# Twelve instead of six tiles normalised ahead in a performer-attention and Fourier-mixing kernel

## The chip, the cores and the metric

The kernel runs on one core of a Trainium2 chip. A core has five engines that each work through their own list of instructions in order: PE (TensorE, matrix products), DVE (VectorE), ACT (ScalarE), POOL (GpSimd) and SP (SyncE, which here issues nearly all DMA transfers). They wait for each other by semaphores. The metric is the device time of one execution in microseconds (us); lower is better.

## The reference

The input is `q`, `k`, `v` of shape (8, 8, 576, 64), all in float32. For each of 64 heads the kernel must compute a linear attention with random features, then join the heads to rows of 512 numbers, and on these 8 x 576 = 4608 rows a Fourier mixing block with a two-layer perceptron:

```python
def phi(x):
    proj = np.einsum('bhsd,md->bhsm', x, omega)
    sq = np.sum(x * x, axis=-1, keepdims=True) / 2.0
    h = proj - sq
    h = h - np.max(h, axis=-1, keepdims=True)
    return np.exp(h) / np.sqrt(m)
q_p, k_p = (phi(q_s), phi(k_s))
kv = np.einsum('bhsm,bhsd->bhmd', k_p, v)
...
X = np.fft.fft(x, axis=1)
X = np.fft.fft(X, axis=2)
u = x + np.real(X).astype(np.float32)
mu = np.mean(u, axis=-1, keepdims=True)
var = np.mean((u - mu) ** 2, axis=-1, keepdims=True)
un = (u - mu) / np.sqrt(var + 1e-06)
ch = np.maximum(un @ w_ch1, 0.0) @ w_ch2
return (u + ch).astype(np.float32)
```

`w_ch1` is 512 x 2048, `w_ch2` 2048 x 512.

## The kernel before, in words

The program has two parts. The **first part** does the attention of 32 pairs of heads, the Fourier transforms of the eight batches (as products with cosine and sine tables), and writes the rows `u` to a DRAM tensor `us`. Beside it the weights are converted, and the first 512 rows ("plain" tiles 0 to 3 of 128 rows) go through the perceptron. The **second part** takes the other 4096 rows in eight blocks of 512, j = 0 to 7, through the perceptron, by Strassen's scheme with seven products instead of eight, applied twice. Blocks 0 and 1 go one by one; from j = 2 (`WIDE`) on they go in pairs. Products of the first layer are at L1710 and L1861, of the second at L2153; the seven operand parts of a weight are called leaves, and they are loaded from DRAM into buffers `wl` (second layer, L2049) or `wx`/`wxw` (first layer). There are twelve such buffers, `NWL`.

Before the first layer a block's rows must be normalised and turned, so that tokens lie along the free dimension. Block 0 does that with PE. For blocks 1 to 7, 28 tiles of 128 rows, it is done without PE: load the tile's rows from `us`, two ACT passes for mean and variance, three small POOL operations, an ACT pass that normalises, a DVE transpose in blocks of 32, and a store to a DRAM tensor `turned`, from which the block is fetched later. The 128 rows of such a tile are every other group of 32 of 256 rows; one DMA fetches them by a rearranged pattern (4 groups of 32 rows).

Where this happens: `normed` (second part, L1094) lists it as steps among the others, by `norm_of` and `by_blocks`, with the row load at L1135 and the store at L1074. Six of the 28 tiles (blocks 1 and half of 2, `EARLY`) are done in the first part by `ahead` (L1571), in buffers `kq` that the attention has left; its row load is at L1578, statistics on ACT at L1582 and L1583, POOL at L1585 to L1587, normalisation at L1589, the transpose on DVE at L1592 and the store at L1594.

The order of all engines is written by a planner, `Listing`. Streams of steps (Python generators) wait for events and buffers; each time one step is chosen and its instructions are issued at the end of its engines' lists. The choice is prescribed by strings: `PICKS` and `BANKS` for all 1853 steps of the first part; `PICKS2` and `BANKS2` for the first 1105 steps of the second part (after these the planner chooses by its own clock); `BANKS` names the PSUM bank of each product. The stages of an `ahead` tile are not steps: `BETWEEN` holds groups of five characters, four digits for a step of the first part and one for a tile, and after that step the tile's next stage is issued. A tile has six stages: load, statistics, POOL, normalisation, transpose, store. The first part ends with the eight products of the second layer of plain tile 3 (L1258); the numbers of its last steps are: 1820 the last eviction that ACT does (L1221), 1822 a DVE sum of the last batch, 1835 to 1838 the sums of block 0's tokens on DVE (L1417), 1841 and 1842 stores of rows, 1845 the store of the mirrored rows, 1846 the load of plain tile 3's rows for the residual, 1847 its addition on DVE (L1271), 1848 its store (L1038), 1849 and 1850 copies of the mirrored rows (L1020), 1853 the end.

In the second part the first product starts with two leaf products on PE (L1710); the third adds into a bank that ACT fills with the result of the first (`seed`, L1742). DVE and POOL start with sums of weight parts (L1666).

Memory of the first part is given back before the second (`early.close()`): the leaf buffers of the second part lie where `kq` and `kqT` were.

Of the kernel before, what the change touches and what calls it, by code (L numbers as in the profile page):

```python
# [18 lines left out]
F32 = mybir.dt.float32  # L19
# [22 lines left out]
class Clock(NamedTuple):  # L42
# [60 lines left out]
PICKS2 = (  # L103
    "0260260270280000270290290290260280240261260290310251280251290450480490270451280230480420480290460440"
    "2802602504812504802404704604504704504505105105103812605105002504102404912404804604604802304404904614"
    "9150048048052053049052053053035044049046037052037041028046125037048044048038046037141154052043043060"
    "0400370330330570540351230450370350360270440580570570470550261230420521230280360360480470400440470300"
    "4603803504004202802905005605614815903905705312305906103405804905003705604905905403304903804803303905"
    "2058048051037033046051034039058051046059059025057046038033052035037055039060057043037047045054057045"
    "0410440670571270670690530670440470400510470510490310600460390270390580380500611280630560590620410631"  # L110
    "2715106104904706000005505005405405604315904004704314403205505305315405303204303805712615102603603914"
    "2052040043038041153049064060053022049050040061039047063000050038040049052050051035129054022059137044"
    "0500500370570320370200630560340480200440500471440590600600410580510360420490400550510520610471510590"
    "6203805106006205606005706015705805406115004216005203215606005915705105205405215604805405204804603815"
    "6027022054049028148047043046051045053155147045047024053148043050153043046148021037047055056052037054"
    "1490480520410430501470540470000551520470520490550571471531560470540440440540520490540480440450490320"
    "5104603503914804704005105103204404604004304904405304704005104303304905013903905005104704005204604804"
    "5051052053053053042145045046054141049046153040052040051051046047051048038053143147049053053053053045"
    "0410450240430430410001460420480270360481410440440380390500420400460440410450420310420480420520500440"
    "4204503804205114903604003804703704004802103904504604701803903905403703605405405205605505503703403705"  # L120
    "2055051051054053050053053050053055036029051050035051050044046048051051050046049053053046052044044034"
    "0440480480450430470240320430460451540460460450500471490550410320400480450450000450460430390470470500"
    "4504604104404002204904004702404504004811804004402104103604704503804004104204203502804804603404504704"
    "6048039039037044045042043044042034034040040045042040040039034000052032033044038033016032040027032037"
    "0340430361250290380400330420320360370480390370460290420300350400500370251260490390170360370330410430"
    "3303103203703603802304403803003604502403603504603303202504604103402304403403103003003202604113814103"
    "3030032041032039026034030029127027131027036029027031041045041027029027034142143032020039037027036028"
    "0270400400261340321270320260310310310370370350340300350300331310350340350390390390391360370260360300"
    "3012903703103103513113903403203303903403703203102903303602902313513402903313602403403203512803513403"
    "2135032036033033133031030034032131030031032032132031034035128032028037032038035132032035032026026023"  # L130
    "0300370161270251270270260360271321331360310250310290351300341311331340241330290350251320320290290180"
    "2002201712503102102403102902402803203401803202803302503203112103012802102102203002802003102302702712"
    "6020023026023023124023020023029017027122028027125024023026128030029024021029027021026023029027020125"
    "0230261210261301330250240240260240220320280220300300251250280220250190250300201200270000200260220220"
    "2303303302602801902612402802702502401902912902802802102702402802002702602502302802102601702502102202"
    "8018027026028020020127127127021018023024019000019025014017026027026018024026017014021016020017020016"
    "022017016025024"
)
BANKS2 = (
    "5670712567365475162765765076736574251742053164735260173564271706573527460152371054362071534267053152"  # L140
    "76"
# [223 lines left out]
def kernel(  # L365
# [667 lines left out]

    outs = out.rearrange("b t d -> (b t) d")
# [61 lines left out]
    def normed(j, pool):  # L1096
        t0 = (NPLAIN * TP + TB * j) // 128

        def paced(i):
            h, k = divmod(i, HT // 128)  # L1100
            before, then = ((("first", j - 1, n[i], 0), "y") for n in ((1, 1, 5, 2), (6, 2, 7, 3)))
            if wide(j):

                n, was = i + TB // 128 * (j - head(j)), head(head(j) - 1)
                order_ = [((("first",) + p), "y") for p in heads(was)]
                at = [m * (len(order_) - 2) // 7 for m in range(8)]
                if j <= WIDE + 1:
                    order_ = [(("first", 0, 7, 0), "y"), *((("second", 0, k), "p1") for k in (4, 6))]
                    order_ += [(("first", 1, ORDER1[k], 0), "y") for k in (0, 2, 4, 6)]
                    at = range(-2, 6)  # L1110
                before, then = order_[at[n]], order_[at[n] + 1]
            yield Step(NONE, after=events_of(range(t0, t0 + TB // 128)) + (before,))
            yield from norm_of(j, t0 + 2 * h, i, pool, None, (h, k), (then,))

        for i in range(TB // 128):
            if (j, i) in EARLY:
                continue
            if wide(j):
                n = i + TB // 128 * (j - head(j))
                was = head(head(j) - 1)  # L1120
                at = 98 * was + 49 * len(unit(was)) * n // 8 - 8
                if j <= WIDE + 1:
                    at = (0, 0, 28, 52, 73, 98, 112, 126)[n]
                yield Fork(paced(i), LEAF * at)
                continue
            yield Fork(paced(i), LEAF * (98 * j - 60 + 8 * i))
# [1203 lines left out]
    def late_turns():  # L2330
        for j in range(2, NTB):
            yield from normed(j, late)
# [36 lines left out]
```

## Time and profile before

| | us |
|---|---|
| median of three runs | 1130.0 (1129.67 to 1130.33) |
| the profiled execution | 1128.43 |
| its span, first to last instruction | 1126.6 |
| PE busy | 1108.2 |
| DVE busy | 888.1 |
| ACT busy | 541.8 |
| POOL busy | 357.4 |

The span is what the profile's views are about; what lies around it in the execution is 1.8 us. Busy times are sums over the engine's instructions. Where a view names a wait as "engine line <- engine line", the first is the one that waited and the second the one whose end let it go. The first product of the second part starts at 421.5 us.

### The profile page before, as it was taken

How to read it: one execution, taken by the hardware profiler on the slowest of the kernel's cores; microseconds unless marked ns; L12 is line 12 of the kernel's file. 1: busy time of each engine (PE TensorE's matmuls, PEld its weight loads, DVE VectorE, ACT ScalarE, POOL GpSimd, SP SyncE). 2: the span in 40 equal slices, each digit the busy share in tenths (PEclk: the TensorE clock that was granted, in tenths of full speed). 3: DMA queues.
4: the chain of work that ended last, by engine and by line, in shares of the span. 5: the costliest groups of instructions: out<-in, count | busy, mean ns of one | idle time of the engine just before them, and what ended most of it. 6: DMA issues, size and time to landing. Idle time of an engine off the chain costs nothing.

```text
span 1126.6 us, 31534 instructions
## 1 busy us (share of the span) xinstructions
PE 1108.2 (98%) x12467; PEld 1000.7 (89%) x12467; DVE 888.1 (79%) x1705; ACT 541.8 (48%) x1644; POOL 357.4 (32%) x381
## 2 busy tenths in 40 slices
PE   8999999999999999999999999999999999999998
PEld 7878888879869779999999889999889999889998
DVE  6999998987577766497788777888667898668895
ACT  7998898856536335534313553223563222341221
POOL 2443443644473335434300454000365000142000
PEclk9999999999999999999999999999999999999999
DMA  8956757565675549799899668757778756556553
GB/s 236 234 178 180 238 174 211 165 206 165 219 234 183 156 137 350 209 292 293 225 317 323 188 204 267 205 151 226 214 208 258 216 152 219 167 156 215 150 157 106
DMA packets 194867, 236.11 MB, mean 210 GB/s; under 512 B 52128, under 2 KB 118944, under 8 KB 194720
## 3 DMA queue, kind: packets, MB, share of 16 engines
q1 hardware_dynamic: 194224, 233.83, 68.3%
q8 instruction: 99, 1.62, 0.6%
q14 instruction: 48, 0.39, 0.1%
q10 hardware_dynamic: 496, 0.26, 0.1%
HBM read 182.13 MB, written 56.10 MB: 211 GB/s over the span
## 4 chain that ended last, share of the span: by engine, by line
PE 90%; DMA 3%; DVE 3%; ACT 2%; SPq 1%; issue 0%; DVEq 0%; ACTq 0%
PE banks L2153 30%; PE banks L1710 27%; PE banks L690 5%; PE banks L1235 5%; PE banks L596 5%; PE banks L1258 5%; PE banks L1861 4%; PE banks L724 3%; PE banks L771 2%; PE banks L933 2%; PE banks L883 1%; DMA wl<-w2l 1%; DMA kq<-in_q_dram 1%; PE banks L893 1%; ACT e L650 1%; PE banks L944 1%
## 5 line engine op out<-in xcount | busy, mean ns | idle before, releaser
L2153 PE MATMUL banks<-wl,sums 128*128 128x128 f32 x1792 | 219.8, 275 | 0.0
L2153 PEld LDWEIGHTS banks<-wl,sums 128*128 128x128 f32 x1792 | 210.9, 192 | 0.9 <-issue 0.2
L650 ACT ACTIVATE e<-banks,nmx 128x128 f32<-128x128 f32 x576 | 165.3, 432 | 22.6 <-DVE nmx L633 22.0
L633 DVE TENSOR_REDUCE nmx<-banks 128x8 f32<-128x1024 f32 (+1 forms) x96 | 89.4, 952 | 19.1 <-PE banks L690 14.9
L2153 PE MATMUL banks<-wl,hid 128*128 128x128 f32 x768 | 99.2, 276 | 3.1 <-DMA wl<-w2l 1.8
L2153 PEld LDWEIGHTS banks<-wl,hid 128*128 128x128 f32 x768 | 92.6, 192 | 4.5 <-DVE part L2129 1.8
L2124 ACT ACTIVATE s<-banks 128x128 f32<-128x128 f32 x112 | 31.0, 277 | 121.1 <-PE banks L2153 111.5
L1710 PE MATMUL banks<-unw,wxw 128*128 128x256 f32 x352 | 85.5, 379 | 0.0
L690 PE MATMUL banks<-om,kqT 64*64 64x128 f32 (+1 forms) x2088 | 79.2, 275 | 1.5 <-ACT kv L740 0.8
L690 PEld LDWEIGHTS banks<-om,kqT 64*64 64x64 f32 (+1 forms) x2088 | 64.5, 138 | 12.7 <-issue 3.4
L2153 PE MATMUL banks<-wl,hx 128*128 128x128 f32 x576 | 74.2, 275 | 0.4 <-DVE part L2129 0.4
L1710 PEld LDWEIGHTS banks<-unw,wxw 128*128 128x128 f32 x352 | 66.6, 190 | 8.9
L1710 PE MATMUL banks<-rx,wxw 128*128 128x256 f32 x288 | 71.2, 379 | 0.0
L1710 PE MATMUL banks<-ttw,wxw 128*128 128x256 f32 x288 | 70.0, 379 | 0.0
L2153 PEld LDWEIGHTS banks<-wl,hx 128*128 128x128 f32 x576 | 69.4, 192 | 0.7 <-DVE part L2129 0.6
L1735 ACT ACTIVATE s<-banks 128x512 f32<-128x512 f32 x65 | 38.6, 595 | 60.0 <-PE banks L1710 54.8
L1235 PE MATMUL banks<-unT,w 128*128 128x128 f32 x512 | 65.4, 279 | 1.7 <-DVE qeT L610 1.7
L1235 PEld LDWEIGHTS banks<-unT,w 128*128 128x128 f32 x512 | 60.2, 192 | 4.5 <-issue 2.3
L539 POOL TENSOR_TENSOR w<-w,raw 128x512 f32<-128x512 f32 x28 | 37.4, 1343 | 76.6 <-DVE raw L533 76.6
L1710 PEld LDWEIGHTS banks<-rx,wxw 128*128 128x128 f32 x288 | 54.5, 190 | 7.3
L1710 PEld LDWEIGHTS banks<-ttw,wxw 128*128 128x128 f32 x288 | 54.5, 190 | 7.3
L1258 PE MATMUL banks<-w,ht 128*128 128x512 f32 x128 | 58.8, 598 | 0.0
(268 smaller groups left out, 2353.3 us busy)
## 6 DMA issues: line engine op xcount, KB each, us to landing
wl<-w2l SPq DMA_DIRECT2D x245, 256.0 KB
wxw<-w1x SPq DMA_DIRECT2D x120, 256.0 KB
raw<-in_moe_w_ch_dram SPq DMA_DIRECT2D x32, 512.0 KB
kq<-in_k_dram SPq DMA_DIRECT2D x32, 288.0 KB
kq<-in_q_dram SPq DMA_DIRECT2D x32, 288.0 KB
vd<-in_v_dram SPq DMA_DIRECT2D x32, 288.0 KB
u<-us SPq DMA_DIRECT2D x30, 256.0 KB
ur<-us SPq DMA_DIRECT2D x30, 256.0 KB
```

What stands on the lines that cost most here:

```text
L539: eng.tensor_tensor(out=dst, in0=dst, in1=lof, op=ALU.add)
L596: nc.tensor.transpose(ps[:, (j - j0) * 128 : (j - j0 + 1) * 128], src(j), ident[:])
L633: nc.vector.tensor_reduce(nmx[:, :, 0:num], pps[:, :, 0 : MF * num].rearrange("p b (c m) -> p b c m", m=MF), axis=AX.X, op=ALU.max, negate ...
L650: nc.scalar.activation(out=e[:, c + (i if num == 1 else 0), :], in_=pps[:, i, MF * c : MF * c + MF], func=AF.Exp, bias=nmx[:, i, c : c + 1],)
L690: nc.tensor.matmul(pps[cols, c, MF * m : MF * m + MF], lhsT=kqT[rows, j, cols], rhs=om2[rows, :],)
L724: nc.tensor.matmul(kvp[cols, i, 0 : D + 1], lhsT=feature(r)[rows, cols], rhs=vds[n % NV][rows, r, :], start=(r == 0), stop=(r == R - 1),)
L1235: nc.tensor.matmul(hp[:, 0:TP], lhsT=w1[:, dc, 128 * fc : 128 * fc + 128], rhs=unTs[key][:, dc, :], start=(dc == 0), stop=(dc == NDC - 1),)
L1258: nc.tensor.matmul(yp[:, 0:DM], lhsT=hs[fc][:, 128 * i : 128 * i + 128], rhs=w2[:, fc, :], start=(fc == 0), stop=(fc == NFC - 1),)
L1710: nc.tensor.matmul(ps[:, span * f : span * f + span].rearrange("f (b q) -> f b q", q=Q), lhsT=left[:, P * f : P * f + P], rhs=right, start ...
L1735: nc.scalar.activation(out=s[:], in_=ps, func=AF.Copy)
L1861: nc.tensor.matmul(cell.rearrange("f t (b q) -> f t b q", q=Q), lhsT=w[:, d, col : col + 128], rhs=right[:, :, d].rearrange("f (t b) q -> ...
L2153: nc.tensor.matmul(ps[:, 0:128], lhsT=left[:, f], rhs=wls[head(j), i, n][:, f], start=start and f == 0, stop=(f == 3), skip_group_check=True,)
```

## The change

- `EARLY` has twelve tiles instead of six: all of blocks 1, 2 and 3. The second part turns only blocks 4 to 7, and the special cases of `normed` for the blocks up to 3 go away.
- An `ahead` tile is put in a `kq` buffer or in one of the three buffers of `kqT` (tag `turned`), as `PLACES` says. `BETWEEN` is new, with 72 entries for 36.
- The row load of a block tile is four DMAs of 32 rows (`load_groups`), in `ahead` and in `norm_of`.
- For the second layer's leaves of blocks 0 and 1, every fifth goes into one of the two `u` buffers or the `turn` buffer, which the second part doesn't use before block 4 is turned: fifteen leaf buffers for twelve.
- `PICKS2` and `BANKS2` are new strings, again of 1105 steps. `PICKS` and `BANKS` stay.

```diff
+PLACES = "kkktttkktttk"
+
 BETWEEN = (
-    "1662016621167001690116910169101693016991169911699117300173011750217502175031766317692176921769317773"
-    "17792177921790317903180341804518204182041820418205182051820518384183851846418465")
+    "1684016841169001690116950169501695016950171011710117101175011750217502175031762417625176361766317664"
+    "1769217692176931769417712177121776317774177751778517853179041790417926180471804818055180551806618066"
+    "1814518145182071820718207182081820818208182261822618377183881842918429184291842918467184681846a1846a"
+    "1846a1846a1846b1846b1846b1846b184791847a1847b184891850a1850b"
+)
...
+    def load_groups(dst, t, k):
+
+        for b in range(4):
+            r = P * t + 32 * (2 * b + k)
+            nc.sync.dma_start(dst[32 * b : 32 * b + 32], us[r : r + 32, :])
...
         if block:
-            rows = us[P * t : P * (t + 2), :].rearrange("(b k q) d -> k b q d", k=2, q=Q)
-            nc.sync.dma_start(u[:], rows[block[1]])
+            load_groups(u[:], t, block[1])
...
-        place = ld.tile([P, 2 * R, D], F32, name="kq", tag="kq")[:].rearrange("p c d -> p (c d)")
+        if PLACES[EARLY.index((j, i))] == "k":
+            place = ld.tile([P, 2 * R, D], F32, name="kq", tag="kq")
+        else:
+            place = att.tile([128, R, 128], F32, name="kqT", tag="turned")
+        place = place[:].rearrange("p c d -> p (c d)")
         u, w = place[:, 0:DM], place[:, DM : 2 * DM]
-        nc.sync.dma_start(u, us[P * t : P * (t + 2), :].rearrange("(b k q) d -> k b q d", k=2, q=Q)[k])
+        load_groups(u, t, k)
...
-    EARLY = [(j, i) for j in (1, 2) for i in range(TB // 128)][:6]
+    EARLY = [(j, i) for j in (1, 2, 3) for i in range(TB // 128)]
...
+    def tag_of(j, i, l):
+
+        n = (49 * j + 7 * order(j).index(i) + PARTS.index(l)) % 15
+        if wide(j) or n % 5 != 4:
+            return "wl", NWL
+        return ("turn", 1) if n == 14 else ("u", 2)
+
...
                 for l in PARTS:
+                    tag, n = tag_of(j, i, l)
                     yield Step(
-                        SP, 0.45, 2.6, take=("wl",), after=(("w2l", i),), kb=165, makes=("wl", j, i, l),
+                        SP, 0.45, 2.6, take=(tag,), after=(("w2l", i),), kb=165, makes=("wl", j, i, l),
...
-                    wl = late.tile([128, 4, 128], F32, name="wl", tag="wl", bufs=NWL)
+                    wl = late.tile([128, 4, 128], F32, name="wl", tag=tag, bufs=n)
...
     def late_turns():
-        for j in range(2, NTB):
+        for j in range(4, NTB):
             yield from normed(j, late)
```

More of the change, by code (lines that the diff above doesn't have):

```diff
@@ L1100, in paced @@
             h, k = divmod(i, HT // 128)
[L1101 to L1111, printed above, removed]
+            n, was = i + TB // 128 * (j - head(j)), head(head(j) - 1)
+            order_ = [((("first",) + p), "y") for p in heads(was)]
+            at = [m * (len(order_) - 2) // 7 for m in range(8)]
+            before, then = order_[at[n]], order_[at[n] + 1]
             yield Step(NONE, after=events_of(range(t0, t0 + TB // 128)) + (before,))
@@ L1115, in normed @@
         for i in range(TB // 128):
[L1116 to L1126, printed above, removed]
+            n, was = i + TB // 128 * (j - head(j)), head(head(j) - 1)
+            yield Fork(paced(i), LEAF * (98 * was + 49 * len(unit(was)) * n // 8 - 8))
     def norm_of(j, t, i, pool, dst, block=None, after=()):
@@ L1595, in ahead @@
         listing.made["turned", j, i] = 0.0
-    EARLY = [(j, i) for j in (1, 2) for i in range(TB // 128)][:6]
+    EARLY = [(j, i) for j in (1, 2, 3) for i in range(TB // 128)]
     def betweens():
         tiles = [ahead(*n) for n in EARLY]
-        return [(int(BETWEEN[n : n + 4]), tiles[int(BETWEEN[n + 4])]) for n in range(0, len(BETWEEN), 5)]
+        return [(int(BETWEEN[n : n + 4]), tiles[int(BETWEEN[n + 4], 16)]) for n in range(0, len(BETWEEN), 5)]
     every = mybir.EngineType
```

75 lines of the change are left out of this document (38 added, 37 removed).

## The prediction

> **What bounds the kernel now.** I read the page's busy times first, then the windows of 30 us, then the waits of PE from 400 us on, and last the timeline of each engine where the two parts of the program meet, at 421 us.
>
> ```profile
> span 1126.6 us, 31534 instructions
> PE 1108.2 (98%) x12467; PEld 1000.7 (89%) x12467; DVE 888.1 (79%) x1705; ACT 541.8 (48%) x1644; POOL 357.4 (32%) x381
> ...
> 480.00:510.00 30.00, 28.23 (x246) 27.50 (x246) 27.73 (x51) 10.06 (x32) 8.61 (x8) 1.00 0.99 292
> 510.00:540.00 30.00, 30.00 (x271) 30.00 (x270) 20.56 (x41) 12.73 (x32) 16.18 (x17) 1.00 0.96 301
> 570.00:600.00 30.00, 28.61 (x248) 28.04 (x247) 25.24 (x49) 5.75 (x23) 0.00 (x0) 1.00 0.99 337
> 1110.00:1140.00 30.00, 12.65 (x111) 12.27 (x110) 6.14 (x14) 2.41 (x9) 0.00 (x0) 0.93 0.18 62
> ...
> PE banks L2153 <- DMA wl<-w2l: 1.8, 3, 0.8
> PE banks L2153 <- DVE part L2129: 1.8, 3, 0.9
> ```
>
> PE is the bound: 1108.2 of 1126.6 us, so only 18.4 us are idle. Of a window's columns the second is PE's busy time, the next four those of PEld, DVE, ACT and POOL, then PE's granted clock and the DMA share. Every window from 360 to 1110 us is full but two: 480 to 510 (1.77 us idle) and 570 to 600 (1.39). The last two lines, the waits from 400 us on, say what is missing there: leaves (`wl`) and DVE's additions. The other 15.2 us lie before 360 us and behind the last matmul; the change leaves the 1853 steps of the first part as they are and adds no matmul, so these stay. More than **3.2 us** is therefore not to be gained.
>
> ```profile
> 408.42 0.63 ACT L1582 ACTIVATE kq<-kq 128x512 bf16<-128x512 f32 x1 [1.49 <-DMA kq<-us]
> 412.58 0.82 ACT L1589 ACTIVATE kq<-kq 128x512 f32<-128x512 f32 x1 [2.59 <-POOL kq L1587]
> 413.31 0.61 ACT L1582 ACTIVATE kq<-kq 128x512 bf16<-128x512 f32 x1
> 416.08 0.82 ACT L1589 ACTIVATE kq<-kq 128x512 f32<-128x512 f32 x1 [1.22 <-POOL kq L1587]
> 422.61 0.58 ACT L1742 ACTIVATE banks<-banks 128x512 f32<-128x512 f32 x1 [5.71 <-PE banks L1710]
> ...
> 416.93 0.71 DVE L1592 STREAM_TRANSPOSE kq<-kq 128x512 f32<-128x512 f32 x1 [2.29 <-ACT kq L1589]
> 421.28 0.69 DVE L1271 TENSOR_TENSOR ur<-ur,banks 128x512 f32<-128x512 f32 x1 [3.64 <-PE banks L1258]
> 421.88 1.26 DVE L1666 TENSOR_TENSOR rx<-w 128x512 f32<-128x512 f32 x1
> ...
> 421.32 2.94 POOL L1666 TENSOR_TENSOR so<-w 128x512 f32<-128x512 f32 x2 [5.28 <-PE banks L1258]
> ...
> 414.67 3.53 SPq L1594 DMA_DIRECT2D turned<-kq  x2
> 422.00 0.36 SPq L1038 DMA_DIRECT2D out_dram<-ur  x1
> 423.88 0.49 SPq L2049 DMA_DIRECT2D wl<-w2l  x1
> ```
>
> This is the seam. Columns: start, duration, engine, line; in brackets the idle time before it. Tiles 4 and 5, the last two of the old six, fill ACT until 416.90; ACT then waits 5.7 us for the second part's first bank. Every engine works its list in order, so what is put at the end of the first part stands before all that the second part does on that engine.
>
> **The gain.** Six tiles less in the second part take away, by the rows above and below, 6 x 0.71 us of DVE, 6 x about 2.4 of ACT, and 6 x 512 KB of transfers (row loads and turned stores) of about 33 MB that the windows from 480 to 600 us move (292, 301, 234 and 337 GB/s x 30 us), at a DMA share of 0.82 to 0.99. Three more leaf buffers let loads run three leaves further ahead of PE. Both help the two stalls; the new order may place the DVE additions better too. Bounds: 0 and -3.2 us. I take **-2.8**, near the upper end, because both causes of waiting are touched.
>
> **Four transfers for one.** 28 block tiles issue 3 more DMAs each. A simple row load takes SP 0.32 to 0.43 us (a leaf 0.32), so 4 x 0.35 = 1.4 us a tile instead of 0.53 to 0.61. That is hidden: SP spends 136.4 us waiting for PE to free leaf buffers in this one trace's leaf loads; without that cover it would be 28 x 0.85 = 24 us of queue. The landing changes more: the old load of tile 4 was issued at 401.68 and ACT could start at 408.42, 6.7 us; a plain load of 128 rows was issued at 392.32 and read at 395.07, 2.75 us. I take 2.7 us for the four.
>
> The Trainium skill (DMA: Bandwidth & Descriptors, "Why a DMA increments its semaphore by 16 and not by 1") has a reason: the number of DMA engines is the largest number up to 16 that divides the slowest dimension of both patterns, which is 4 for the old form and 16 for 32 rows. The two rows agree with it. The same page ("Rules for kernel authors") speaks against the split: small transfers should be joined, as below 64 KB one pays mostly overhead. By it the loads land no sooner than now, which is the fourth rival below.
>
> **The seam.** BETWEEN tells after which step of the first part each of a tile's six stages is issued. New tiles 7 and 8 have nearly the places of old 4 and 5: statistics, POOL chain and normalisation after step 1820, ACT's last eviction. Tiles 9, a and b come on top: four stages of 9 after step 1842; then the stores of 7 and 8, and four stages each of a and b after 1846; the three transposes after 1847 (the addition at 421.28); the stores of a and b after 1850, the second last SP step.
>
> One tile on ACT, from statistics to normalised: 413.31 to 416.90 = 3.59 us, POOL's 1.09 within, during which ACT waits in order. Tiles 7 and 8 end at 416.90 as 4 and 5 did. Tile 9's rows come before; it ends at 416.90 + 3.59 = 420.5. Tile a's loads stand on SP behind the store of tile 8, which needs the transpose that ends at 417.64: store until 418.2, four issues until 419.6, landed by about 422.0; tile a ends at 425.6, tile b (landed meanwhile) at **429.2**. Only then ACT starts the second part: 429.2 - 422.61 = 6.6 us late. The last transpose ends at 429.9, so DVE's first sum is 8.0 us late; POOL is free at about 428.4, 7.1 late. PE has two leaf products without ACT, from 421.5 to 423.5; its third needs the bank that ACT seeds. So PE stands, 6.6 us. Behind the waiting ACT are seeds and saves, behind DVE the sums of weights and the additions, behind SP the first leaf loads and the stores of `rx`; PE waits for all these.
>
> Bounds: if every row were there in time, five tiles from the end of the last eviction (406.93) end at 406.93 + 5 x 3.59 = 424.9, 2.3 us late, of which a product that needs no seed (1.73 us, L1861) could cover part: +0.6. At the other end the first leaf buffers lie on the memory of the places, so SP's first leaf load waits until tile b's store has landed: issued at 430.5, + 2.7 = 433.2, against 423.88: +9.3. I take **+6.6**, since the order on ACT, DVE and SP is fixed by the code.
>
> **Earlier tiles.** Tiles 4, 5 and 6 add 3 x (1.56 + 0.82) = 7.1 us to ACT between 390 and 407 us, where ACT idled 6.4 us. Evictions of hidden blocks come up to 2 us later; PE takes the bank of one of them again 2 us after its release. Bounds 0 and +2; I take **+0.3**.
>
> Sum: -2.8 + 6.6 + 0.3 = **+4.1 us** on the profiled execution's 1128.4 (span 1126.6 + 1.8 around it). The median of the runs is 1130.0, 1.6 higher; with the same step it becomes 1134.1, forecast **1134**.
>
> **Rivals.**
> The seam holds (faster): ACT's 5.7, DVE's 3.6 and POOL's 5.3 us of idleness there, and an order of the second part that gives PE other work first, take the three tiles in; the two stalls close: 1130.0 - 3.0 = 1127. For it: idle time on three engines at once. Against: three tiles of 3.59 us are 10.8 us in a row on ACT. Decides: whether the first seed stands by about 424 us. Chance 0.19.
> Both small (no change): the seam near 3 us, the gain 3: 1130. Chance 0.18.
> The gain does not come: DMA share stays near 1 at 480 to 600 us because leaves are its larger part, and the stalls only move: 1130.0 + 6.6 + 0.3 = 1137. For it: the leaf loads are 256 KB each and outnumber the row loads. Chance 0.13.
> The four transfers land no sooner than the one (slower): tile a's rows come 6.7 instead of 2.7 us after their issue, so that the seam costs 10.6: 1138. For it: four completions instead of one. Against: the plain load's 2.75 us. Chance 0.04.
> PE slows after standing still: a stop of 6.6 us is longer than any in this trace (longest 2.8 us, granted clock 1.00), and the only window with a lower clock, 0.93, is that in which PE has ended. At half clock for some 3 us PE does 1.5 us less work: 1134 + 1.5 = 1135.5. Chance 0.08. The Trainium skill (TensorE: Matmul & The Clock Gate, "Part 1: The HAM clock gate") states such a gate, half clock after an idle window of about 3.4 us and the same time to come back; no row here is long enough to show it.
>
> **Chances.** Forecast 0.38, and 0.13, 0.04 and 0.08 that are slower too: slower 0.63; same 0.18; faster 0.19. "Same" is within 0.2%, 1127.7 to 1132.3, about what a measurement of this kernel can tell from no change. The forecast's own range is 1132.3 to 1138; that for 8 in 10 goes down into the first rival and up to the seam's upper end (1130.0 + 9.3 + 0.3 = 1139.6): 1127.2 to 1139.5.
>
> **What would show it.** Right: PE idle 5 us or more between 421 and 435 us, its wait put down to ACT's seed or to the tiles' stages; the last normalisation in a place ending near 429; the windows at 480 and 570 us nearly full; ACT's wait on `kq<-us` gone or short. Wrong: PE full from 415 to 440 us; tile b ending before 424; or the stalls at 480 to 600 us unchanged.

## The result and the profile after

| | before | after |
|---|---|---|
| median on one chip, us (six runs each) | 1130.05 (1128.91 to 1132.69) | 1137.66 (1136.05 to 1139.39) |
| span of the profiled execution | 1126.6 | 1135.9 |
| ratio after / before | | 1.0069, 95% interval 1.0055 to 1.0083 |

The kernel became slower by 7.6 us; the forecast was 1134, with a range of 1127.2 to 1139.5. Line numbers are now those of the kernel after: the seed is still L1742, `s` is L1735, row loads are L1044, plain second layer L1254, washing products L2281, leaf loads L2057, second-layer products L2161.

The profile after: the page's busy times, and the three windows of 30 us that matter (second column PE busy, last but two its clock).

```profile
PE 1111.1 (98%) x12467; PEld 1003.1 (88%) x12467; DVE 890.1 (78%) x1684; ACT 540.6 (48%) x1644; POOL 389.8 (34%) x402
...
420.00:450.00 30.00, 20.21 (x108) 17.31 (x107) 11.85 (x14) 13.90 (x29) 15.35 (x18) 0.83 0.79 259
480.00:510.00 30.00, 29.45 (x242) 28.52 (x241) 24.18 (x36) 7.12 (x25) 9.71 (x7) 1.00 0.86 251
570.00:600.00 30.00, 29.71 (x266) 29.52 (x266) 28.14 (x46) 4.76 (x21) 6.17 (x5) 1.00 1.02 304
```

The two old stalls shrink from 1.77 + 1.39 = 3.16 us of idle PE to 0.55 + 0.29 = 0.84, and a new hole of 9.79 us stands at the seam, at a lower clock: 8.85 us in one wait, and 0.82 in one for POOL at 444.7. PE's busy time is 2.9 us longer for the same 12467 matmuls: some of them ran slowly.

The seam on its engines' timelines (start, duration, engine, line; in brackets the idle time before it and what ended it):

```profile
415.43 0.81 ACT L1589 ACTIVATE kq<-kq 128x512 f32<-128x512 f32 x1 [4.08 <-POOL kq L1587]
424.96 0.63 ACT L1582 ACTIVATE kqT<-kqT 128x512 bf16<-128x512 f32 x1 [1.60 <-DMA kqT<-us]
431.23 0.81 ACT L1589 ACTIVATE kq<-kq 128x512 f32<-128x512 f32 x1 [1.22 <-POOL kq L1587]
431.95 0.58 ACT L1742 ACTIVATE banks<-banks 128x512 f32<-128x512 f32 x1
435.56 0.60 ACT L1735 ACTIVATE s<-banks 128x512 f32<-128x512 f32 x1 [3.03 <-PE banks L1710]
435.59 0.69 DVE L1666 TENSOR_TENSOR rx<-w 128x512 f32<-128x512 f32 x1 [2.80 <-DMA turned<-kq]
...
421.56 1.72 SPq L1044 DMA_DIRECT2D kqT<-us  x4
432.82 0.55 SPq L1594 DMA_DIRECT2D turned<-kq  x1
...
432.58 2.08 PE L1710 MATMUL banks<-unT,w 128*128 128x128 f32 x8 [8.85 <-ACT banks L1742]
434.45 1.91 PE L1710 MATMUL banks<-tt,w1s 128*128 128x128 f32 x8
```

From top: the normalisation of tile 7 starts at 415.43 (8 and 9 follow at 419.04 and 422.54); tile a's rows, issued from 421.56 on, can be read at 424.96; tile b is normalised by 432.04, and in the same breath ACT seeds the bank PE has waited 8.85 us for. There is a second end 3.5 us behind: tile b's store, issued at 432.82, has landed when SP issues the first leaf loads (435.53), ACT writes its first `s` (435.56; `s` is a product's result that ACT copies out of its bank) and DVE starts its first sum (435.59). The view puts ACT's wait down to PE, but that product had ended at 434.66; DVE's line names the store. PE hardly waits for this second end, because it needs 2.08 and 1.91 us for two leaf products that take 1.06 elsewhere.

### The profile page after: what moved, and what is told of

Read it like the earlier page. It is cut to its first block, busy times and chain, and to the rows that moved or that the text cites. A ratio compares the mean times of both kernels' runs of the same rounds, so it can differ in the third digit from the quotient of the medians.

```text
span 1135.9 us, 31674 instructions
## 1 busy us (share of the span) xinstructions
PE 1111.1 (98%) x12467; PEld 1003.1 (88%) x12467; DVE 890.1 (78%) x1684; ACT 540.6 (48%) x1644; POOL 389.8 (34%) x402
## 4 chain that ended last, share of the span: by engine, by line
PE 86%; DVE 4%; DMA 4%; ACT 3%; issue 1%; SPq 1%; POOL 1%; DVEq 0%; ACTq 0%; POOLq 0%
PE banks L2161 30%; PE banks L1710 26%; PE banks L1231 5%; PE banks L696 4%; PE banks L602 4%; PE banks L1861 3%; PE banks L1254 3%; PE banks L730 2%; PE banks L777 2%; PE banks L939 2%; PE banks L889 1%; ACT e L656 1%; DVE nmx L639 1%; DMA raw<-in_moe_w_ch_dram 1%; PE banks L899 1%
## 5 line engine op out<-in xcount | busy, mean ns | idle before, releaser
L2161 PE MATMUL banks<-wl,sums 128*128 128x128 f32 x1792 | 219.8, 275 | 0.5 <-issue 0.5
L2161 PEld LDWEIGHTS banks<-wl,sums 128*128 128x128 f32 x1792 | 210.6, 192 | 1.6 <-issue 0.9
L2161 PE MATMUL banks<-wl,hid 128*128 128x128 f32 x768 | 99.1, 275 | 0.3 <-DVE part L2137 0.3
L2161 PEld LDWEIGHTS banks<-wl,hid 128*128 128x128 f32 x768 | 92.9, 192 | 0.9 <-DVE part L2137 0.5
L2161 PE MATMUL banks<-wl,hx 128*128 128x128 f32 x576 | 74.2, 275 | 0.4 <-DVE part L2137 0.4
L1735 ACT ACTIVATE s<-banks 128x512 f32<-128x512 f32 x65 | 38.5, 596 | 69.4 <-PE banks L1710 64.3
L2161 PEld LDWEIGHTS banks<-wl,hx 128*128 128x128 f32 x576 | 69.4, 192 | 0.8 <-DVE part L2137 0.6
L2210 POOL TENSOR_TENSOR more<-more,part 128x512 f32<-128x512 f32 x2 | 2.6, 1313 | 176.3 <-ACT part L2203 176.3
```

Source lines behind the costliest of these rows:

```text
L1735: nc.scalar.activation(out=s[:], in_=ps, func=AF.Copy)
L2161: nc.tensor.matmul(ps[:, 0:128], lhsT=left[:, f], rhs=wls[head(j), i, n][:, f], start=start and f == 0, stop=(f == 3), skip_group_check=True,)
```

## The experiments

Differences between two of these kernels are worked out from their ratios to the kernel before, which ran on the same chip beside each (medians there 1128.9 to 1129.9). The intervals of such a difference are the two ratios' intervals, added in quadrature.

### Three tiles without their chains

```diff
         load_groups(u, t, k)
         yield
+        if EARLY.index((j, i)) >= 9:
+            for _ in range(4):
+                yield
+            nc.sync.dma_start(turned_of(j, h)[:, :, k], u.rearrange("p (g x) -> p g x", g=4))
+            listing.made["turned", j, i] = 0.0
+            return
```

> The changed kernel, but tiles 9, a and b are only loaded and stored as they are: their statistics, POOL chain, normalisation and transpose are left out (so three tiles of block 3 stay unnormalised); the transfers and their places stay. Theory (the three chains in a row on ACT hold up the second part): ACT reaches its first seed at about 423 us instead of 431.95, PE stands under 1.5 us there, no half clock, and the time is that of the change without its seam: 1137.7 - 8.8 (the stop) - 2.0 (half clock) = about 1127, range 1125.5 to 1128.5. Rival 1 (the new order of the second part or the fifteen buffers are what costs): the time stays above 1134. Rival 2 (SP's queue, which still holds the late loads and stores, is what holds the second part): the stop shrinks by less than half, 1131 to 1134.

Measured: 1137.61 us (1136.62 to 1138.68), ratio 1.0073 [1.0052, 1.0094]: no gain at all. That felled the narrow form of my theory, that three tiles in a row on ACT are the loss. Timelines of this kernel (its lines stand six further on):

```profile
422.94 1.76 SPq L1044 DMA_DIRECT2D kq<-us  x4
427.94 0.57 SPq L1583 DMA_DIRECT2D turned<-kq  x1
...
422.23 0.58 ACT L1748 ACTIVATE banks<-banks 128x512 f32<-128x512 f32 x1 [2.80 <-PE banks L1716]
434.23 0.60 ACT L1741 ACTIVATE s<-banks 128x512 f32<-128x512 f32 x1 [11.42 <-DMA turned<-kq]
```

ACT seeds the bank at 422.23, in good time. But the next thing it writes, `s`, waits for tile b's store (`turned<-kq`), and this lands only at 434.2: its rows were loaded from 422.94 on, the store was issued at 427.94 behind two transfers of 512 KB (`us<-uh`), and the queue had to move these first. PE stood 9.8 us for `s` in place of 8.8 for the seed. So the seam has two ends of nearly one length, and taking one away shows the other.

### PE kept busy through the stop

```diff
-        for h in range(2):
+        for h in [0, 1] * (37 if i == 2 else 1):
```

This adds 72 small products into a bank that nobody reads, ahead of the seed.

> The changed kernel with 72 more of the washing products (identity, 128 x 256, into the bank that is washed anyway) on PE between its second and third leaf product, so that PE works through most of the 8.85 us stop. Nothing else changes. Theory (PE at half clock after the stop is a cost of its own): granted clock 1.00 from 420 to 440 us, the first leaf products behind the stop take 1.06 instead of 2.08 us, and the time falls by 1.5 to 2.2 us, to 1135.5 to 1136.2. Rival (ACT, DVE and POOL are the bound there anyway, so a faster PE only waits again): clock 1.00, but time unchanged within 0.5 us, 1137.2 to 1138.2.

Measured: 1136.67 us (1136.49 to 1137.08), ratio 1.0065 [1.0045, 1.0085]: 1.0 us below after by the medians and 0.5 +/- 2.8 by the ratios, so not clear of zero, and below what was expected for the clock. PE's waits at the seam in this kernel:

```profile
PE banks L1710 <- ACT s L1735: 1.6, 1, 1.6
PE banks L1710 <- ACT banks L1742: 1.0, 1, 1.0
```

The clock was 1.00 all the time and the leaf products took 1.06 to 1.16 us again. What PE gained so it spent on waiting for `s`, thus for tile b's store. This kernel's profile was 0.95 us ahead of after's already when PE's wait for the seed ended (431.63 for 432.58), and it is no more than that ahead two products of L1861 later (439.63 for 440.58). The slow clock was real, but it hid behind the second end.

### One transfer for the rows, in the kernel after

```diff
-        for b in range(4):
-            r = P * t + 32 * (2 * b + k)
-            nc.sync.dma_start(dst[32 * b : 32 * b + 32], us[r : r + 32, :])
+        rows = us[P * t : P * (t + 2), :].rearrange("(b k q) d -> k b q d", k=2, q=Q)
+        nc.sync.dma_start(dst, rows[k])
```

> The changed kernel with its row loads of block tiles as one transfer by the rearranged pattern, as before the change. Theory (four transfers land sooner, and at the seam that counts): tile a's rows land 6.7 instead of 3.4 us after their issue, ACT's wait on them grows by 2 to 3.5 us, and the time goes up by as much: 1139.5 to 1141.5. Rival (the landing is hidden, SP's shorter issue of 0.55 instead of 1.76 us makes up for it): 1136.5 to 1138.5.

Measured: 1141.57 us (1139.13 to 1142.74), ratio 1.0102 [1.0076, 1.0127], 3.7 +/- 3.3 us above after (3.9 by the medians), in the direction expected: ACT waited 4.17 us for tile a's rows in place of 1.60, and PE 11.9 us for the seed in place of 8.85.

### Other places for the same twelve tiles

Everything of after stays but the string `BETWEEN`:

```diff
 BETWEEN = (
-    "1684016841169001690116950169501695016950171011710117101175011750217502175031762417625176361766317664"
-    "1769217692176931769417712177121776317774177751785317853179041790417926180471804818055180551806618066"
-    "1814518145182071820718207182081820818208182261822618377183881842918429184291842918467184681846a1846a"
-    "1846a1846a1846b1846b1846b1846b184791847a1847b184891850a1850b"
+    "1684016841169001690116950169501695016950171011710117101173021730317304173051730117322173231732217334"
+    "1733517382175331754617546176941769517696176931769417695177121771217713177131771417714177151771517776"
+    "17787177881790617906179091790a1790b179271806718207182081820818209182091820a1820a1820b1820b1820818209"
+    "1820a1820b1838718388183891838a1838b1846718468184691846a1846b"
 )
```

The loads of tiles 2 to 5 go after step 1730, those of 9, a and b after 1790; tiles 2 to 6 are normalised by 1777; the statistics of 8, 9, a and b follow each other after 1820, and then their four normalisations, so that POOL's part of one tile runs beside ACT's of the next; all five transposes after 1838 and all five stores after 1846, ahead of the copies `us<-uh` after 1849.

> The changed kernel with other places for the twelve tiles, all else equal: loads of tiles 2 to 5 before the row load of block 0, their statistics in ACT's idle time between 377 and 388 us, tiles 7 to b loaded by about 408 us and on ACT side by side (statistics of all, then normalisations), so that the last normalisation should end near 418 us. Theory (only the seam costs; the rest of the change gains 2 to 3 us): PE's stop at 423 us is gone, the clock stays at 1.00, 1130.0 - 2.5 = 1127.5, range 1126 to 1129.5, faster than the kernel before. Rival 1 (ACT has no room for six more tiles before 422 us): the stop shrinks but stays over 3 us, 1131 to 1135. Rival 2 (earlier ACT work delays the attention or block 0 and opens new gaps of PE between 370 and 420 us): no stop at the seam, but 1130 or more.

Measured: 1127.10 us (1125.19 to 1130.34), ratio 0.9980 [0.9968, 0.9992]. This is faster than both kernels, and 0.0089 +/- 0.0018 of a ratio (10.1 +/- 2.1 us) faster than after, with the same tiles, transfers, buffers and steps. So the loss lies in the places. That it beats the kernel before rests on the timed runs alone, 2.3 us [0.9, 3.6]: from 360 us on PE is idle for as long in one profile as in the other, 3.1 us, here 2.3 of it at the seam and 0.3 between 480 and 600 us. Its window at the seam, and ACT's last normalisation, seed and first `s`:

```profile
420.00:450.00 30.00, 27.71 (x156) 24.26 (x154) 18.40 (x19) 12.87 (x23) 22.46 (x15) 1.00 0.92 323
...
415.61 0.81 ACT L1589 ACTIVATE kq<-kq 128x512 f32<-128x512 f32 x1 [0.36 <-POOL kq L1587]
421.84 0.58 ACT L1742 ACTIVATE banks<-banks 128x512 f32<-128x512 f32 x1 [5.42 <-PE banks L1710]
424.43 0.60 ACT L1735 ACTIVATE s<-banks 128x512 f32<-128x512 f32 x1 [2.00 <-DMA out_dram<-ur]
```

The last tile is done 5.4 us ahead of the seed. Four statistics in a row, then four normalisations, take ACT about 2.4 us a tile (406.76 to 416.42 for four) where the kernel after waits through POOL's part of each, 3.6 us a tile.

### Four transfers in the kernel before

Only the row loads of before are changed, to the four of after.

> The kernel before, with the row loads of all block tiles in four transfers of 32 rows and nothing else changed. The kernel after with one-transfer loads took 3.9 us more than after, which I put down to its last two tiles being loaded where PE already stands. Before has no tile there: its PE waits for no row load in the whole second part (only 1.8 us for leaves and 1.8 us for DVE). So theory: no difference, 1129.5 to 1130.5 beside 1130; the rows land sooner and nobody waits for them. Rival: the transfers alone are worth something (the two stalls at 480 and 570 us fall in the stretch in which the second part loads rows): 1128 or less. Second rival: three more issues for each of 28 tiles keep leaves back on SP: 1131.5 or more.

Measured: 1127.38 us (1122.13 to 1131.33), ratio 0.9982 [0.9963, 1.0000]. Between the theory (no difference) and the rival (faster): the interval just touches 1, and the two profiled spans are equal, 1126.6 us. A small gain is possible; a loss of 1.5 us by SP's extra issues, the second rival, is excluded.

### Earlier loads, and the three raw tiles again

Three kernels: after with only the loads of 9, a and b moved ahead (steps 1804, 1815, 1823, the first at which their buffers are given back); the raw tiles with these loads; the raw tiles with their stores ahead of `us<-uh` too (all of them after step 1846). The strings of the first:

```diff
 BETWEEN = (
...
-    "1769217692176931769417712177121776317774177751785317853179041790417926180471804818055180551806618066"
-    "1814518145182071820718207182081820818208182261822618377183881842918429184291842918467184681846a1846a"
-    "1846a1846a1846b1846b1846b1846b184791847a1847b184891850a1850b"
+    "1769217692176931769417712177121776317774177751785317853179041790417926180471804818049180551805518066"
+    "1806618145181451815a18207182071820718208182081820818226182261823b18377183881842918429184291846718468"
+    "1846a1846a1846a1846b1846b1846b184791847a1847b184891850a1850b"
```

> After with only the loads of tiles 9, a and b at earlier places (9 after step 1804, a after 1815, b after 1823, as soon as their buffers are free); statistics, normalisations, transposes and stores stay where they are. Theory (two chains end at nearly the same time: the normalisations in a row on ACT, and the late loads with their stores): with the rows there in time, tile a's statistics follow tile 9's normalisation at 423.3 instead of 424.96, so tile b is normalised by 430.4 instead of 432.0 and its store lands at about 433.9 instead of 435.6. Time 1135.5 to 1136.5, 1 to 2 us less than after. Rival (the late loads alone are the cause): 1131 or less. Rival (SP's order is filled by the early loads, and what they displace is late): 1137.5 or more.

Measured: 1140.61 us (1139.31 to 1140.93), ratio 1.0094 [1.0074, 1.0114]. The last rival, that what the loads displace is late, held. The row on ACT did become shorter, as the theory said: the seed comes at 428.82 instead of 431.95. But the output's store and the copies `us<-uh` go out 2.2 to 2.3 us later, the last tile's store stands behind them, and ACT's first `s` waits for it until 438.22 instead of 435.56. PE stands 7.1 us for the seed and 5.8 for `s`.

> The three tiles again only loaded and stored (their statistics, POOL chain, normalisation and transpose left out), with the early loads of the run beside it. With late loads this took 1137.6, as PE stood 9.8 us until tile b's store had landed at 434.2: the late tiles of the second part lie on the memory of its place. Theory: the stores of a and b are now issued at about 424 instead of 427.2 to 428.5, but still behind the two transfers of 512 KB from uh to us (1 MB at 200 to 250 GB/s, 4 to 5 us), so they land at about 430 to 431: PE stands 5.5 to 6.5 us and the time is 1133 to 1134.5. Rival (only the late loads matter, the stores are quick): 1127 to 1129. Rival (neither matters): 1137.

Measured: 1140.64 us (1139.49 to 1142.23), ratio 1.0098 [1.0079, 1.0117]; none of the three forecasts.

> The same, and the stores of 9, a and b too at an earlier place (after step 1846, ahead of the two transfers from uh to us). What is left out is as in the run beside it. Theory: all stores are issued by 421.5 and land at about 424, so that PE goes on within 1 us of where it did before: 1126.5 to 1128.5. With the three raw runs in a ladder (late loads and stores 1137.6; early loads about 1134; early loads and stores about 1127.5) the memory handed over by the last store is shown to be a second chain as long as the normalisations. Rival (tiles 7 and 8, also later than the last two of before, hold the seam): 1131 or more.

Measured: 1134.26 us (1131.62 to 1136.57), ratio 1.0044 [1.0026, 1.0062]; the number of its rival, but for another reason. What I had overlooked shows on SP and DVE of the middle kernel (raw tiles, early loads):

```profile
SPq L1044 <- DMA turned<-kq: 2.0, 1, 2.0
...
424.80 0.67 SPq L1038 DMA_DIRECT2D ur<-us  x1
...
428.81 0.69 DVE L1267 TENSOR_TENSOR ur<-ur,banks 128x512 f32<-128x512 f32 x1 [7.76 <-DMA ur<-us]
```

A load put right behind the store that frees its buffer makes SP wait until that store has landed, twice 2.0 us here (the other wait, for `turned<-kqT`, is as long), and each tile adds 1.70 us of issues. All that follows on SP moves: the load `ur<-us` goes out at 424.80 where after issues it at 417.27, and DVE's last addition of the first part comes at 428.81, with the output's store behind it. I had moved the loads past a full queue without counting it. These runs therefore don't size the late loads by themselves; what they show is a third end of the first part, SP's own order. The step from the middle kernel to the last one moves only the stores: 0.0054 +/- 0.0026 of a ratio, 6.1 +/- 3.0 us. Two things change by it. The last store no longer stands behind the output's store and the copies on SP, and is issued at 428.85 instead of 432.58; and it lands 4.1 instead of 6.3 us after its issue.

### The three tiles left out

Tiles 9, a and b get nothing at their places in after; the store of tile 1 is issued three times more, early, into the memory of their results.

> After with tiles 9, a and b left out of the first part altogether: no load, statistics, normalisation, transpose or store at their places; instead the store of tile 1 is issued three times more, some 35 us before the seam, to the memory of their results (so the output is not the reference's). The raw runs left the loads and stores in the queue and gained nothing; here the queue is free of them too. Theory (the three tiles' queue entries and memory are the loss, not tiles 4 to 8 and not the changed order of the second part): tile 8's store is issued at about 420.6 and lands by about 423.5, PE stands 0 to 2 us, 1126.5 to 1129. Rival (tiles 7 and 8, normalised 2.9 us later than the last two of before, hold the seam as well): 1131 to 1134. Rival (the second part's new order needs what the old one did not, and starts late for itself): 1135 or more.

Measured: 1124.51 us (1123.38 to 1127.18), ratio 0.9956 [0.9943, 0.9970], 0.0113 +/- 0.0019 of a ratio or 12.8 +/- 2.2 us less than after. Its seam (window and seed; the first `s` follows at 423.33):

```profile
420.00:450.00 30.00, 29.32 (x164) 25.77 (x163) 20.39 (x21) 14.10 (x25) 24.00 (x16) 1.00 0.88 310
...
422.44 0.58 ACT L1751 ACTIVATE banks<-banks 128x512 f32<-128x512 f32 x1 [2.82 <-PE banks L1719]
```

Tiles 7 and 8, as late here as in after, do little harm by themselves, and so does the second part's order: PE is idle 0.68 us in this window.

### Only two stores behind the 1 MB

From the better places, the stores of a and b are moved from after step 1846 to after 1850, as after has them.

```diff
-    "1820a1820b1838718388183891838a1838b1846718468184691846a1846b"
+    "1820a1820b1838718388183891838a1838b1846718468184691850a1850b"
```

> The re-planned places (1127.1 beside 1129.9 of before), with one thing moved: the stores of tiles a and b go after step 1850, behind the two transfers of 512 KB from uh to us, where after has them, instead of after 1846, ahead of them. Nothing waits longer on ACT, POOL or DVE. Theory (the late tiles' memory is handed over when the last store has landed, and a store lands only when the 1 MB issued before it on the queue has moved): the stores are issued at about 423 instead of 420.2 to 421.4 and land at about 428.5 to 429.5 instead of 424; PE stands 4 to 5 us more, 1131 to 1132.5. Rival (only the normalisations in a row on ACT matter, which end at 416.4 here): 1127 to 1127.5.

Measured: 1133.46 us (1132.06 to 1135.03), ratio 1.0038 [1.0024, 1.0052], 0.0058 +/- 0.0018 or 6.5 +/- 2.1 us above the better places; the theory's direction, a little more than its 4 to 5.

```profile
429.43 0.60 ACT L1735 ACTIVATE s<-banks 128x512 f32<-128x512 f32 x1 [7.07 <-DMA turned<-kq]
430.08 2.07 PE L1710 MATMUL banks<-unT,w1s 128*128 128x128 f32 x8 [5.44 <-ACT s L1735]
```

The last store is issued at 423.70 instead of 420.18, since SP comes to it only behind the output's store and the copies, and it lands 5.6 instead of 4.0 us after its issue, at 429.4 instead of about 424. So of the 5.1 us some 3.5 are SP's order and 1.6 the slower landing. PE stands 5.44 us in place of 0.38, and begins again with a product of twice the length: the slow clock adds to it.

### One transfer, and twelve leaf buffers, at the better places

The first is the edit shown above; the second lets every leaf take the next of twelve buffers:

```diff
-                    wl = late.tile([128, 4, 128], F32, name="wl", tag=tag, bufs=n)
+                    wl = late.tile([128, 4, 128], F32, name="wl", tag="wl", bufs=NWL)
```

> The re-planned places with one transfer for the rows of a tile instead of four. In after this cost 3.9 us. Here the rows of 9, a and b are read 1 to 4 us after their issue, and the last normalisation ends at 416.4, about 5 us ahead of the second part's first seed. Theory (the four transfers are worth what the seam waits for them): rows that land up to 4 us later are partly covered, 1127 to 1129.5. Rival (they are worth the same at any place): 1131. Rival (three issues less for each of 28 tiles free SP, and it is faster): 1126.5 or less.

Measured: 1134.65 us (1132.22 to 1137.65), ratio 1.0047 [1.0031, 1.0064]: 7.6 +/- 2.3 us above the better places, more than in after and more than either case expected. The cost is not at the seam. The longest of PE's waits from 360 to 428 us (three more of 0.9 to 1.9 us have `y`, `ht` and `unT` as their releasers), and the window from 390:

```profile
PE banks L889 <- ACT y L912: 2.9, 1, 2.9
...
390.00:420.00 30.00, 23.91 (x178) 19.24 (x179) 19.99 (x56) 19.62 (x55) 13.67 (x27) 1.00 0.53 164
```

Here the statistics stand early on ACT, ahead of evictions (`y`, `ht`) that PE needs. When the rows come late, ACT stands ahead of their statistics (8.6 us in two waits, put down to issue, and 7.9 us in five, to the loads; with four transfers 5.2 us, all put down to loads), the evictions behind it wait too, and PE loses 6.1 us in a window that was full.

> The re-planned places with twelve leaf buffers as in before: every leaf takes the next of the twelve in turn, in the order of issue of after. The forecast's gain of 2.8 us was put down to six tiles less in the second part and to three more buffers, together. Theory (both): the leaf stalls come back in part, 1.8 us for leaves in before: 1128 to 1129.5. Rival (the tiles and the order alone did it): 1126.5 to 1127.6. If it is 1130 or more, the order of the second part needs the fifteen.

Measured: 1130.23 us (1127.74 to 1133.40), ratio 1.0006 [0.9991, 1.0021]: 2.9 +/- 2.2 us above fifteen buffers. The median is just inside the case in which the order needs the fifteen, and the interval reaches back over the theory's. PE waits 2.4 us for leaves, which it doesn't at all with fifteen, and runs at half clock for 3.4 us behind the longer of the two waits:

```profile
PE banks L2161 <- DMA wl<-w2l: 2.4, 2, 2.1
```

## Why the prediction was right, and where it was off

**What bounds the kernel, and the direction.** Right: the seam costs more than the stalls give back, and the order of places on in-order engines does it. The other places show it: nothing else changed, and the sign did.

**The sum.** It was -2.8 + 6.6 + 0.3 = +4.1. The two profiles give -2.3 for the stalls and about +12.2 for the seam, together +9.9, where their spans differ by 9.3; the timed difference is 7.6. The seam's cost lies above the upper bound given for it. That the time still fell into the range, near its upper end, is owed to the range's width (its upper end took the seam's bound and no gain at all), not to the size that was forecast. Two rivals named the nearest numbers, but their grounds fail: the gain came (1137 supposed that it did not), and the four transfers landed sooner (1138 supposed that they did not).

**The gain, -2.8 of at most -3.2.** By the windows it was 3.16 - 0.84 = 2.3 us. By timed runs the kernel without the three tiles is 5.0 us [3.4, 6.4] below before, though its profiled span is only 2.9 below. That kernel also does three tiles' work less, and the kernel with better places, which does all of it, is 2.3 us [0.9, 3.6] below before; so the bound of 3.2 is not refuted. But it was made from one execution, 1.6 us faster than the median, and even in the first 360 us, where PE's order is the same, PE is idle for 9.1 to 11.3 us in the fourteen profiles here. The three buffers matter: without them 2.9 +/- 2.2 us are lost, and fewer tiles alone don't stop the leaf waits. How much of that is the buffers and how much an order written for fifteen stays open.

**The seam, +6.6 with bounds +0.6 and +9.3.** This is the term that was mis-sized. At the seam PE loses 9.79 us of idleness and about 2.4 us by three leaf products at a low clock (2.08 + 1.91 + 1.63 against 3 x 1.06), 12.2 together, beyond my upper bound; the kernel without the three tiles is 12.8 +/- 2.2 us faster. Term by term:

- *The row on ACT*: forecast to end at 429.2, it ended at 432.04. Its rhythm was right (tile 7 to 8 to 9 at 3.6 and 3.5 us, a and b at 3.5, and a wait of 1.6 us for tile a's rows, forecast 1.5). But it began 2.85 us late, at tile 7: the rows were there at 409.78 against 408.42 for old tile 4 (1.36 us), since SP came to the load at 404.48 and took 3.65 us for its four issues, where the old one was issued at 401.68 (`BETWEEN` has it after step 1804 instead of 1803, so that it stands behind two more issues, and the stores of earlier tiles hold SP up by some 1.5 us; I had compared only the places of the later stages); and POOL's first small operation took 2.61 us in place of 1.11 (1.5 us).
- *The store of the last tile*: I had its mechanism (leaf memory is handed over when tile b's store lands) but used it as an upper bound at 433.2. It is the second end of the seam, at 435.5, and holds by itself: it alone kept the kernel with raw tiles at 1137.6. In after it is issued on an empty queue and is late because tile b is. What I never considered is that such a store can stand behind the output's store and 1 MB of copies, worth 6.5 +/- 2.1 us at the better places.
- *The clock*, a rival with 0.08: it came together with the forecast, not in its place. Worth about 2.4 us on PE, but no gain clear of zero in time without it (0.5 +/- 2.8 us).

**Earlier tiles, +0.3.** Right for ACT and PE in this kernel: PE is full from 360 to 420 us. But the earlier tiles also delay tile 7's load on SP, and that is paid at the seam. With one transfer and early places the same neighbourhood cost 7 us, so the cover named (ACT's idle time) holds only as long as the rows land quickly.

**Four transfers.** That the rows land no sooner (0.04) is refuted: one transfer costs 3.7 +/- 3.3 us in after and 7.6 +/- 2.3 at the better places. The rule of the Trainium skill weighed against it (DMA: Bandwidth & Descriptors, "Rules for kernel authors": join small transfers) is not borne out for these row loads, which are of 64 KB each, at the edge of what that rule calls small: four of 64 KB land in 1.9 to 2.6 us each by the issue-to-landing column, and a reader gets its rows sooner than from one of 256 KB. The page's other rule ("Why a DMA increments its semaphore by 16 and not by 1"), 4 engines for the old form and 16 for 32 rows, would explain it; no run here isolates it.

**The faster rival, 0.19**, named its deciding point well: the first seed by about 424 us. In after it came at 431.95; at the better places it came at 421.84, and that kernel ran in 1127.1, the time that rival gave. Its two parts are not quite as that rival had them: the stalls give back 2.9 us there, and the seam still has 2.3 us of idle PE.

**Not settled:** what after's late loads cost by themselves, since moving them alone disturbed SP; and whether the gain of four transfers in before (0 to 0.4%) is real.

## What to carry to other kernels

Where one part of a program hands its engines and memory to the next, list every end: the last instruction on each in-order engine, SP's queue with its issues and waits, and the landing of the last store that reads the memory to be reused, including what stands ahead of it on SP and on the DMA queue. Removing one end shows only the next, so test by taking the whole work out first, and then single ends from a version that has the others in order. Work slipped into another engine's idle time belongs in batches (all statistics, then all normalisations) and far enough ahead for its store to land, but never where its operands may be late: an in-order engine makes everything behind it wait for them.

## What the runs showed of the hardware

- **PE's clock after a stop.** In five-microsecond windows of after (second column PE busy, then PEld, DVE, ACT, POOL, the clock):

```profile
425.00:430.00 5.00, 0.00 (x0) 0.00 (x0) 0.71 (x1) 3.71 (x9) 0.94 (x3) 0.70 0.81 244
430.00:435.00 5.00, 2.42 (x11) 2.42 (x12) 0.71 (x1) 1.31 (x3) 0.94 (x3) 0.50 0.69 206
435.00:440.00 5.00, 5.00 (x29) 4.65 (x29) 4.26 (x5) 1.65 (x4) 2.77 (x2) 0.78 0.69 215
```

  PE stopped at 423.7. A mean of 0.70 means half clock from about 427.0, 3.3 us later; it went on at 432.58, and the mean of 0.78 means full clock from about 437.2, 4.6 us later. In the other kernels with such stops the way back, worked out in the same way, took between 3.9 us (one transfer) and 5.8 (raw tiles, early loads). What is constant is the grid: the spells at half clock last 10.24 us here, 6.83 with the two stores moved back, 13.66 with one transfer and 17.07 with raw tiles and early loads, that is 3, 2, 4 and 5 times 3.41. And a short stop can be enough: with twelve buffers a stop of 2.13 us, and with four transfers in before one of 1.45 us at 582.0, were followed by one spell of 3.41 us, while a stop of 2.79 us near the start of before, ended at 9.92, left the clock at 1.00. (Each of the two short stops has one of 0.28 us shortly ahead of it.) The Trainium skill (TensorE: Matmul & The Clock Gate, "Part 1: The HAM clock gate") gives a free-running window of some 3.4 us, at least one of them idle before half clock and one busy before full clock. The grid agrees; that a whole window must be idle does not, by the stops of 1.45 and 2.13 us.

- **A small POOL operation can take fourteen times as long.** The same operation on 128x1 numbers in after:

```profile
411.44 2.61 POOL L1585 TENSOR_SCALAR kq<-kq 128x1 f32<-128x1 f32 x1 [5.76 <-ACT kq L1583]
430.10 0.19 POOL L1585 TENSOR_SCALAR kq<-kq 128x1 f32<-128x1 f32 x1 [2.39 <-ACT kq L1583]
```

  From 411.44 on DVE ran additions of two tensors without a gap; at 430.10 it stood still. The same two durations return in other kernels here (2.66 and 0.19, 2.72 and 0.19). The Trainium skill (SBUF — State Buffer, "Who interferes with whom") says that a DVE instruction with two SBUF inputs contends with a GpSimd one that reads SBUF, which fits; no run here varied DVE's load alone.

- **A store's landing depends on what was issued before it.** Tile b's store of 256 KB took 2.6 us from issue to landing on an empty queue (after; the DMA share is 0.02 in the microsecond from 433), 4.0 behind four other stores (better places), and 5.6 and 6.1 behind two transfers of 512 KB (the two stores moved back; raw tiles).
